# Rows of x as pairs of rounded products with 128 stationary columns, and smaller loads of q, k and v per step

## Chip, cores and metric

One core of a Trainium2 chip runs the whole kernel in one launch. The metric is the device time of a run in microseconds (us). The kernel before was timed in three runs, and one further execution was profiled.

## What is computed

Talking-heads attention over 8 batches, 12 heads, 448 positions and 64 values per head, whose output, laid out as 3584 tokens of 768 values (x), goes through a mixture of 8 experts with one expert chosen for each token:

```python
scores = scale * np.matmul(q, k.transpose(0, 1, 3, 2))
scores = np.einsum('bhij,hg->bgij', scores, w_pre)
scores = scores - np.max(scores, axis=-1, keepdims=True)
attn = np.exp(scores)
attn = attn / (np.sum(attn, axis=-1, keepdims=True) + 1e-09)
attn = np.einsum('bhij,hg->bgij', attn, w_post)
attn_out = np.matmul(attn, v)
x = attn_out.transpose(0, 2, 1, 3).reshape(B * S, H * D)
logits = x @ w_gate
expert_idx = np.argmax(logits, axis=1)
gate_w = softmax(logits)[np.arange(N), expert_idx]
out[expert_idx == e] = gate_w * (np.maximum(xe @ w1[e], 0.0) @ w2[e])
```

## The kernel before

**Two stages.** Attention fills the first 690 us or so and the experts the rest. The attention stage goes over 32 tiles (T) of 120 queries, four to a batch (120, 120, 120 and 88 queries). A tile is cut into blocks of 20 queries, 6 to a tile and 5 to the short one, so there are 184 blocks (NU), 23 to a batch. The program is unrolled in steps u = 0 to 183, one block to a step. A table, `steps`, says which piece of work is issued in which step and stage, and ORDER (L773) gives the order of the stages inside a step. Every engine takes its instructions in that order, SP's and POOL's queues of transfers included.

**One block.** relayout (L286) brings 20 queries of all heads onto 120 partitions by two transfers, two steps ahead. mix (L293) multiplies with w_pre on PE into two PSUM banks (bank_m). maxima (L306) reduces each bank on DVE, and powers (L313) takes the exponentials on ACT with the sums, two instructions and two read-outs. One step later recip (DVE) and weigh (L329, POOL) make w_post divided by the sums, in a buffer wp with three copies. Two steps later post (L338) multiplies with it on PE and turns the block, and evict_p copies it on DVE.

**One tile.** load_q (L125) brings the queries with two transfers, and split_q rounds them to fp32r on ACT (the high part) and subtracts the rounded from the whole on POOL (the low part); load_k and split_k do the same to the keys of the next batch. An fp32r value keeps fewer bits, and PE multiplies it in one go; a product of high and low parts stands for a full one. qk (L260) makes the scores from three such products. av and av_side (L378 to L413) multiply with v, evict_side (ACT) and evict_x (L415, DVE) add the two parts up to x transposed: XT, 128 partitions (two heads) by three chunks by 120 tokens, for each half g of the heads.

**Rows of x.** rows (L425) turns XT round. For each of the six chunks of 128 values, the chunk is the stationary operand (128 x 120 or 128 x 88, fp32), and the moving one is xg, 136 columns: the identity, which gives the tokens as rows, and the 8 columns of w_gate that belong to the chunk, which gives the chunk's share of the logits. evict_r (L433) copies each half, 408 columns, on ACT, store_x writes the rows to the table XD in DRAM with one transfer for each half, and choose (L454) adds the six shares of the logits on DVE and looks for the largest. Its followers (mark, rank, gate, place, token, number, scatter) put the token's number into the list of its expert.

The steps that matter to the change are set in the lines L680 to L756: for the tile before the current one, av in step u0 + 3 and u0 + 5, evict_x one step after each, rows in step u0 + n + 1 (rsteps, n blocks in the current tile), evict_r one later. Loads of q, k and v are issued from L696, L706 and L708. Just ahead of the steps, constants_last (L230) fills constants on POOL; keep_clock (L189) gives PE products of no use to the result while it waits at the start and at the end of the stage.

**Experts.** For each expert, the tokens of its list are gathered from XD, turned and split, and hidden (L1120) and result (L1140) multiply in fp32r with w1 and w2, 512 or 384 moving columns to a product, 128 stationary ones. The change doesn't touch them. patch (L527), at the end of the attention stage, makes four products of 128 stationary columns and a single moving one.

## Time and profile before

| | |
|---|---|
| median of 3 runs | 1230.86 us (1229.25 to 1233.55) |
| the profiled execution | 1217.47 us |
| its span, first to last instruction | 1215.8 us |
| PE busy | 1184.5 us (97%), 19433 matmul records |
| weight loads of PE busy | 995.1 us (82%) |
| DVE, ACT, POOL busy | 798.6, 721.6, 393.4 us |
| TensorE clock granted, mean | 0.994 of full speed |
| moved by DMA | 211.19 MB, 178761 packets |

The profile is of one execution. PE stands for the matmuls, PEld for the loads of their stationary operand, which can go on beside a matmul. One fp32 product stands as two matmul records with a load each, an fp32r product as one. Records of consecutive matmuls overlap, since each is counted to the end of its pipeline: how fast they follow one another is read from starts, and the busy time tells only that PE had something in flight.

### The profile page before, as it was taken

What the parts mean: (1) busy time and instruction counts of PE and PEld (TensorE: products, weight loads), DVE (VectorE), ACT (ScalarE), POOL (GpSimd) and SP (SyncE); (2) the same over time, 40 slices, a digit from 0 to 9 for tenths busy, and PEclk for the clock granted to TensorE, in tenths of its full rate; (3) what the DMA queues carried; (4) which work ended last, traced back from release to release, by engine and by line L of the source; (5) the groups of instructions that cost most, each with busy time, mean ns of one, the idle gap of its engine ahead of it and who ended that gap; (6) DMA issues with size and microseconds to landing.
All of it is one profiled execution on the core that took longest, in us unless ns stands there. A gap on an engine that the chain in (4) does not pass through costs nothing. (4 is left out here: it accounts for less than half of the span.)

```text
span 1215.8 us, 46340 instructions
## 1 busy us (share of the span) xinstructions
PE 1184.5 (97%) x19433; PEld 995.1 (82%) x19433; DVE 798.6 (66%) x1992; ACT 721.6 (59%) x1485; POOL 393.4 (32%) x613
## 2 busy tenths in 40 slices
PE   7999999999999999999999899999999999999996
PEld 3677787777777778777777798898989899989886
DVE  5787888878888878788789745454535344545320
ACT  5777777877777868787776444444434344444220
POOL 5443553534544435445435312020202002110100
PEclk9999999999999999999999999999999999999998
DMA  7566657566656575576556377575555647574300
GB/s 205 191 189 191 200 162 217 181 178 204 204 166 207 157 223 182 171 209 202 175 176 192 108 229 205 166 204 159 181 154 152 170 130 216 166 221 135 120 20 34
DMA packets 178761, 211.19 MB, mean 174 GB/s; under 512 B 85541, under 2 KB 156213, under 8 KB 178536
## 3 DMA queue, kind: packets, MB, share of 16 engines
q1 hardware_dynamic: 172342, 183.93, 51.4%
q0 software_dynamic: 6064, 23.86, 5.6%
q8 instruction: 164, 2.69, 0.9%
q14 instruction: 61, 0.50, 0.1%
q10 hardware_dynamic: 130, 0.22, 0.0%
HBM read 97.59 MB, written 23.07 MB: 99 GB/s over the span
## 5 line engine op out<-in xcount | busy, mean ns | idle before, releaser
L317 ACT ACTIVATE et<-bm,st 124x448 f32<-124x448 f32 x360 | 225.4, 631 | 148.7 <-DVE st L309 123.4
L309 DVE TENSOR_REDUCE st<-bm 124x1 f32<-124x448 f32 x360 | 208.6, 620 | 74.3 <-PE bm L303 68.2
L350 PEld LDWEIGHTS bp<-wp,et 64*64 64x64 f32 (+1 forms) x10052 | 197.0, 135 | 70.0 <-issue 44.8
L1130 PE MATMUL pm_h<-si,ah 128*128 128x512 f32 (+1 forms) x768 | 230.2, 381 | 3.2 <-DVE si L632 2.1
L368 DVE COPY pt<-bp 128x480 f32<-128x480 f32 x352 | 213.6, 649 | 2.4 <-PE bp L350 2.1
L334 POOL TENSOR_SCALAR wp<-Wpost,st 124x60 f32<-124x60 f32 x360 | 151.6, 436 | 164.6 <-DVE st L327 129.1
L350 PE MATMUL bp<-wp,et 64*64 64x60 f32 (+1 forms) x10052 | 190.7, 218 | 0.3 <-issue 0.3
L303 PE MATMUL bm<-sb,Wquad 60*60 60x448 f32 (+3 forms) x1408 | 185.2, 561 | 5.2 <-ACT et L317 5.1
L1130 PEld LDWEIGHTS pm_h<-si,ah 128*128 128x128 f32 x768 | 143.2, 188 | 29.1 <-issue 3.4
L280 ACT COPY si<-bs 120x896 f32<-120x896 f32 (+1 forms) x187 | 159.8, 910 | 6.2 <-PE bs L270 5.8
L1130 PE MATMUL pm_h<-si,al 128*128 128x512 f32 (+1 forms) x384 | 146.0, 380 | 0.0
L1134 DVE SCALAR_TENSOR_TENSOR hl<-pm_h,hh 128x512 fp32r<-128x512 f32 (+1 forms) x64 | 42.1, 658 | 142.7 <-ACT hh L1133 142.6
L410 PE MATMUL bs<-pt,vt 128*64 128x120 f32 (+1 forms) x2496 | 132.5, 262 | 1.2 <-DVE pos L509 1.2
L410 PEld LDWEIGHTS bs<-pt,vt 128*64 128x64 f32 x2496 | 120.0, 138 | 5.3 <-ACT ah L574 1.4
L1133 ACT ACTIVATE hh<-pm_h 128x512 fp32r<-128x512 f32 (+1 forms) x64 | 36.6, 572 | 146.4 <-PE pm_h L1130 146.4
L1150 PE MATMUL pm_y<-bh,hh 128*128 128x384 f32 x480 | 122.1, 334 | 1.3 <-DVE y L1155 1.3
L1150 PE MATMUL pm_y<-bl,hh 128*128 128x384 f32 x480 | 121.8, 334 | 0.0
L148 POOL TENSOR_TENSOR ql<-qr,qh 128x360 fp32r<-128x360 f32 (+1 forms) x78 | 69.8, 905 | 160.9 <-ACT qh L147 123.1
L1150 PE MATMUL pm_y<-bh,hl 128*128 128x384 f32 x480 | 121.8, 334 | 0.0
L648 POOL DMA_INDIRECT si<-XD,tcl x28 | 39.1, 1397 | 254.0 <-DVE y L1155 241.0
L1159 POOL DMA_INDIRECT out<-y,ti x30 | 31.1, 1038 | 184.7 <-ACT y L1157 77.7
L1150 PEld LDWEIGHTS pm_y<-bh,hh 128*128 128x128 f32 x480 | 86.8, 188 | 2.1 <-DVE y L1155 1.6
(170 smaller groups left out, 1723.6 us busy)
## 6 DMA issues: line engine op xcount, KB each, us to landing
sb<-si SPq DMA_DIRECT2D x343, 210.0 KB
wraw<-in_w SPq DMA_DIRECT2D x48, 512.0 KB
wraw<-in_w SPq DMA_DIRECT2D x64, 384.0 KB
vt<-in_v SPq DMA_DIRECT2D x64, 192.0 KB
kr<-in_kT SPq DMA_DIRECT2D x42, 224.0 KB
qr<-in_qT SPq DMA_DIRECT2D x48, 180.0 KB
XD<-xr SPq DMA_DIRECT2D x48, 180.0 KB
sb<-si SPq DMA_DIRECT2D x16, 189.0 KB
```

What stands on the lines that cost most here:

```text
L148: engine.tensor_sub(out=lo, in0=src, in1=hi.bitcast(F32))
L280: copy(out=SI[T][:ni, 2 * c:2 * c + 2, :], in_=bank[:ni, :, :S])
L303: nc.tensor.matmul(out=bank_m[r][CUT[c], :S], lhsT=Wquad[CUT[r], CUT[c]], rhs=sb[CUT[r], c, :], start=True, stop=True)
L309: nc.vector.reduce_max(out=st[:R1, 0, c:c + 1], in_=bank_m[c][:R1, :S], axis=AX.X, negate=True)
L317: nc.scalar.activation(out=et[:R1, c, :], in_=bank_m[c][:R1, :S], func=AF.Exp, bias=st[:R1, 0, c:c + 1], scale=1.0, accum_out=st[:R1, 1, c ...
L334: nc.gpsimd.tensor_scalar(out=wp[:R1, c, :], in0=Wpost[:R1], scalar1=st[:R1, 2, c:c + 1], scalar2=None, op0=ALU.mult)
L350: nc.tensor.matmul(out=banks[r][col * JC:(col + 1) * JC, at_:at_ + W], lhsT=et[CUT[r], n, kg * JC:(kg + 1) * JC], rhs=wp[CUT[r], n, :], st ...
L368: nc.vector.tensor_copy(out=flat[:, :, i0 + r * IB:i0 + (r + 1) * IB] .rearrange("p x (n k) -> p x n k", k=IQ), in_=banks[r][:, :2 * NJ * ...
L410: nc.tensor.matmul(out=HOME[T, g][r * D:(r + 1) * D, p, :], lhsT=VV[b][:, c, h * D:(h + 1) * D], rhs=PT[T][:, c, h, :ni], start=(c == 0), ...
L1130: nc.tensor.matmul(out=ph[:, :n], lhsT=wx[:, fs], rhs=xx, start=(m == 0), stop=(m == 3 * NK1 - 1))
L1134: nc.vector.scalar_tensor_tensor(out=hl[:, ft, :n], in0=ph[:, :n], scalar=0.0, in1=hh[:, ft, :n].bitcast(F32), op0=ALU.max, op1=ALU.subtract)
L1150: nc.tensor.matmul(out=py[g][:, :384], lhsT=hx[:, kt, ts], rhs=wx[:, g * 384:(g + 1) * 384], start=(n == 0), stop=(n == 3 * NK2 - 1))
```

## The change

rows of a tile becomes twelve fp32r products in place of six fp32 ones, for the tiles in PARTED (29 of 32). split_r rounds XT to a high part on ACT and subtracts it on POOL to a low part. Both lie in buffers with eight columns more than the three chunks need, so that a chunk always gives 128 stationary columns. The moving operand xp holds, for two chunks, the identity between the high and low parts of w_gate: 144 columns meet the high part of x, 136 the low part, and both add up in PSUM. A sheet so has 432 columns in place of 408, the rows of two chunks lie side by side in it, and choose adds 96 values for each token in place of 48. To make room, idle has 256 columns in place of 512 with twice as many products, and wp two copies in place of three. load_q comes in two parts in two steps, and loads of k and v are put into other steps; xg, which the three last tiles still use, gets its identity in step 38.

```diff
+XW = P + 2 * NE
-    def load_q(T):
+    def load_q(T, part):
         b, it, ni = geom[T][:3]
-        qr = q_p.tile([P, NPAIR, IT], F32, name="qr", bufs=1)
+        if part == 0:
+            QR[T] = q_p.tile([P, NPAIR, IT], F32, name="qr", bufs=1)
+        cs = slice(part * 3, part * 3 + 3)
...
-            nc.sync.dma_start(out=qr[half * D:(half + 1) * D, :, :ni], in_=src[half])
-        QR[T] = qr
+            nc.sync.dma_start(out=QR[T][half * D:(half + 1) * D, cs, :ni], in_=src[half][:, cs])
...
-    idle = const.tile([P, 512], BF16, name="idle")
+    idle = const.tile([P, 256], BF16, name="idle")
+    xp = r_p.tile([P, NPAIR // 2, 2 * XW - P], F32R, name="xp")
+    XH = [[r_p.tile([P, 3 * IT + 8], F32R, name=f"x{x}{g}") for x in "hl"] for g in range(2)]
...
-        for _ in range(n):
-            nc.tensor.matmul(out=bank, lhsT=idle[:, :P], rhs=idle, start=True, stop=True)
+        for _ in range(2 * n):
+            nc.tensor.matmul(out=bank[:, :256], lhsT=idle[:, :P], rhs=idle, start=True, stop=True)
...
     def constants_last():
-        for c in range(NPAIR):
-            nc.gpsimd.tensor_copy(out=xg[:, c, :P], in_=ident)
+        for p in range(NPAIR // 2):
+            nc.gpsimd.tensor_copy(out=xp[:, p, 2 * NE:XW], in_=ident)
+            for c, (hi, lo) in zip((2 * p, 2 * p + 1), ((NE, 0), (XW, XW + NE))):
+                hi, lo = (xp[:, p, x:x + NE] for x in (hi, lo))
+                nc.vector.tensor_copy(out=hi, in_=xg[:, c, P:XG])
+                nc.vector.tensor_sub(out=lo, in0=xg[:, c, P:XG], in1=hi.bitcast(F32))
+        for x in XH[0] + XH[1]:
+            nc.vector.tensor_copy(out=x[:, 3 * IT:], in_=step.to_broadcast([P, 8]))
...
+    def constants_late():
+        for c in range(NPAIR):
+            nc.gpsimd.tensor_copy(out=xg[:, c, :P], in_=ident)
...
-        wp = e_p.tile([P, 2, H * IQ], F32, name="wp")
+        wp = e_p.tile([P, 2, H * IQ], F32, name="wp", bufs=2)
...
+    def split_r(T, g):
+        ni = geom[T][2]
+        xt = XT.pop((T, g))
+        xh, xl = (x[:, :3 * IT].rearrange("p (c i) -> p c i", i=IT)[:, :, :ni] for x in XH[g])
+        nc.scalar.copy(out=xh, in_=xt[:, :, :ni])
+        nc.gpsimd.tensor_sub(out=xl, in0=xt[:, :, :ni], in1=xh.bitcast(F32))
+
     def rows(T, g, bank):
         ni = geom[T][2]
+        if T in PARTED:
+            SHEET[T, g] = bank[:ni, :3 * XW]
+            for c in range(3):
+                p, odd = divmod(3 * g + c, 2)
+                whole = xp[:, p, odd * 2 * NE:odd * 2 * NE + XW]
+                out = bank[:, c * XW:(c + 1) * XW]
+                cols = slice(0, XG) if odd else slice(NE, XW)
+                xh, xl = (x[:, c * IT:c * IT + P] for x in XH[g])
+                nc.tensor.matmul(out=out, lhsT=xh, rhs=whole, start=True, stop=False)
+                nc.tensor.matmul(out=out[:, cols], lhsT=xl, rhs=whole[:, cols],
+                                 start=False, stop=True)
+            return
...
     def store_x(T, halves=(0, 1)):
...
+        if T in PARTED:
+            ps = slice(2 * halves[0], 2 + halves[-1])
+            nc.sync.dma_start(
+                out=XD[1 + t0:1 + t0 + ni, 2 * P * ps.start:2 * P * ps.stop]
+                .rearrange("t (p x) -> t p x", x=2 * P),
+                in_=XF[T][:ni].rearrange("t (p x) -> t p x", x=2 * XW)[:, ps, 2 * NE:2 * XW - 2 * NE])
+            return
...
+    PARTED = {T for T in rsteps if rsteps[T] <= NU - 9}
...
-            at(max(up - 1, 0), "load", load_q, T)
             for part in range(2):
+                at(max(up - 1, 0) + part, "load", load_q, T, part)
...
-            for part, k in enumerate((16, 17, 19, 20, 22, 24, 25, 27)):
+            for part, k in enumerate((8, 14, 18, 19, 20, 21, 24, 25)):
                 at(u0 + k, "load", load_v, b + 1, part)
-            for c in range(NPAIR):
-                at(U - 18 + 2 * c, "load", load_k, b + 1, c)
+            for c, k in enumerate((6, 7, 9, 11, 13, 15)):
+                at(U - 23 + k, "load", load_k, b + 1, c)
...
             at(vs[g] + 1, "vec", evict_x, T, g)
+            if T in PARTED:
+                at(vs[g] + 1, "early", split_r, T, g)
...
+    at(38, "scatter", constants_late)
```

Three places of the order in which the engines get their instructions. PE, the step in which the first tile's rows are made; before, six fp32 products in one row (bs is a PSUM bank, xt the transposed x, xg the identity with w_gate):

```order
L350 MATMUL bp_106<-wp,et 64x60 x2
L350 MATMUL bp_107<-wp,et 64x60 x2
L430 MATMUL bs_103<-xg,xt 120x136 x6
L303 MATMUL bm_104<-sb_124,Wquad 64x448
L303 MATMUL bm_104<-sb_124,Wquad 60x448
```

The same place now (xh and xl are the high and low part, L457 and L458 the two products):

```order
L365 MATMUL bp_109<-wp,et 64x60 x2
L365 MATMUL bp_110<-wp,et 64x60 x2
L457 MATMUL bs_106<-xp,xh_131 128x144
L458 MATMUL bs_106<-xp,xl_132 128x136
L457 MATMUL bs_106<-xp,xh_131 128x144
L458 MATMUL bs_106<-xp,xl_132 128x136
L457 MATMUL bs_106<-xp,xh_131 128x144
L458 MATMUL bs_106<-xp,xl_132 128x136
L457 MATMUL bs_106<-xp,xh_133 128x144
L458 MATMUL bs_106<-xp,xl_134 128x136
L457 MATMUL bs_106<-xp,xh_133 128x144
L458 MATMUL bs_106<-xp,xl_134 128x136
```

Twelve products take the place of six, between the same neighbours. DVE, from the last copies of the start to the first maximum; before:

```order
L228 MEMSET bp_106 128x512
L228 MEMSET bp_107 128x512
L280 COPY si<-bs_102 120x896
L309 TENSOR_REDUCE st<-bm_104 124x1
L309 TENSOR_REDUCE st<-bm_105 124x1
L325 TENSOR_SCALAR st<-st 124x2
```

Now, from the last of six pairs of small instructions on (the first five pairs read the same):

```order
L240 CAST xp<-xg 128x8
L241 TENSOR_TENSOR xp<-xg,xp 128x8
L243 CAST xh_131<-step 128x8
L243 CAST xl_132<-step 128x8
L243 CAST xh_133<-step 128x8
L243 CAST xl_134<-step 128x8
L324 TENSOR_REDUCE st<-bm_107 124x1
L324 TENSOR_REDUCE st<-bm_108 124x1
L340 TENSOR_SCALAR st<-st 124x2
```

Sixteen instructions stand ahead of the first maximum that did not stand there. POOL, over two steps in which keys are split and x is split too; before:

```order
L334 TENSOR_SCALAR wp<-Wpost,st 124x60 x2
L122 TENSOR_TENSOR kl<-kr,kh 128x448
L334 TENSOR_SCALAR wp<-Wpost,st 124x60 x4
L122 TENSOR_TENSOR kl<-kr,kh 128x448
L549 DMA TB<-tg,di 28672x2
```

and now:

```order
L349 TENSOR_SCALAR wp<-Wpost,st 124x60 x2
L124 TENSOR_TENSOR kl<-kr,kh 128x448
L445 TENSOR_TENSOR xl_132<-xt,xh_131 128x360
L349 TENSOR_SCALAR wp<-Wpost,st 124x60 x4
L124 TENSOR_TENSOR kl<-kr,kh 128x448
L445 TENSOR_TENSOR xl_134<-xt,xh_133 128x360
L599 DMA TB<-tg,di 28672x2
```

The subtraction for x stands behind that for the keys, and ahead of the scatter.

## Rows read from the trace of the kernel before

**Rows 1.** Busy us of each engine (count), PE clock, DMA share, GB/s; attention.
```profile
300.00:400.00 100.00, 99.99 (x2550) 78.95 (x2546) 84.45 (x252) 77.83 (x189) 48.10 (x82) 1.00 0.64 194
```
**Rows 2.** Timeline of PE, one step: start us, us, engine, line, operation, count.
```profile
393.79 1.08 PE L303 MATMUL bm<-sb,Wquad 64*64 64x448 f32 x8
394.59 1.09 PE L350 MATMUL bp<-wp,et 64*64 64x60 f32 x56
...
395.70 1.63 PE L430 MATMUL bs<-xg,xt 128*120 128x136 f32 x12
397.26 0.98 PE L303 MATMUL bm<-sb,Wquad 64*64 64x448 f32 x8
```
**Rows 3.** Timeline of ACT over the same and the next step.
```profile
389.93 0.58 ACT L121 CAST kh<-kr 128x448 fp32r<-128x448 f32 x1
392.51 0.64 ACT L317 ACTIVATE et<-bm,st 124x448 f32<-124x448 f32 x1 [2.00 <-DVE st L309]
...
396.76 0.20 ACT L317 ACTIVATION_READ_ACCUMULATOR et<-bm,st 124x1 f32 x1
...
397.75 0.93 ACT L437 COPY xr<-bs 120x408 f32<-120x408 f32 x2
398.58 0.57 ACT L121 CAST kh<-kr 128x448 fp32r<-128x448 f32 x1
399.09 0.64 ACT L317 ACTIVATE et<-bm,st 124x448 f32<-124x448 f32 x1
```
**Rows 4.** Groups by line and form: count, busy us, mean ns, idle us before.
```profile
L430 PE MATMUL bs<-xg,xt 128*120 128x136 f32 x288 | 39.3, 286 | 0.1
...
L430 PEld LDWEIGHTS bs<-xg,xt 128*120 128x120 f32 x288 | 34.6, 183 | 0.9
```
**Rows 5.** Timeline of PE's weight loads in the rows step.
```profile
395.68 1.44 PEld L430 LDWEIGHTS bs<-xg,xt 128*120 128x120 f32 x12
```
**Rows 6.** Timeline of PE, two experts: first and last start of 21 and of 23 triples.
```profile
702.97 0.51 PE L1130 MATMUL pm_h<-si,ah 128*128 128x384 f32 x2
...
715.11 0.34 PE L1130 MATMUL pm_h<-si,ah 128*128 128x384 f32 x1
...
1149.72 0.62 PE L1130 MATMUL pm_h<-si,ah 128*128 128x512 f32 x2
...
1164.36 0.39 PE L1130 MATMUL pm_h<-si,ah 128*128 128x512 f32 x1
```
**Rows 7.** The products of patch(): ns min/median/max of a load; their timeline.
```profile
L530 PEld LDWEIGHTS bs<-edge,et x4: 186/190/192, 685.0 to 685.4; 120*128 120x128 f32 x4
...
685.02 0.52 PEld L530 LDWEIGHTS bs<-edge,et 120*128 120x128 f32 x4 [1.68 <-DVE si L632]
```
**Rows 8.** Groups by line and form: fp32r weight loads of the experts.
```profile
L1150 PEld LDWEIGHTS pm_y<-bh,hh 128*128 128x128 f32 x480 | 86.8, 188 | 2.1 <-DVE y L1155 1.6
```
**Rows 9.** Groups by line and form: roundings on ACT, a subtraction on POOL.
```profile
L122 POOL TENSOR_TENSOR kl<-kr,kh 128x448 fp32r<-128x448 f32 x42 | 48.4, 1153 | 0.0
...
L147 ACT CAST qh<-qr 128x360 fp32r<-128x360 f32 x48 | 39.7, 827 | 6.6 <-DMA qr<-in_qT 3.9 <-DMA sb<-si 2.8
```
**Rows 10.** Timeline of DVE, the step before the rows step.
```profile
390.87 0.53 DVE L419 TENSOR_TENSOR xt<-bs,xt 128x360 f32<-128x360 f32 x1
```
**Rows 11.** Timeline of POOL, the same step.
```profile
391.73 1.14 POOL L122 TENSOR_TENSOR kl<-kr,kh 128x448 fp32r<-128x448 f32 x1
393.32 1.05 POOL L549 DMA_INDIRECT TB<-tg,di  x1 [0.45 <-DVE tg L544]
394.75 0.84 POOL L334 TENSOR_SCALAR wp<-Wpost,st 124x60 f32<-124x60 f32 x2 [0.39 <-PE bm L303]
```
**Rows 12.** Timeline of DVE at the start of the steps.
```profile
21.21 1.16 DVE L309 TENSOR_REDUCE st<-bm 124x1 f32<-124x448 f32 x2 [1.42 <-PE bm L303]
...
23.45 0.17 DVE L327 RECIPROCAL st<-st 124x2 f32<-124x2 f32 x1
```
**Rows 13.** Groups by line and form: loads of the mix, and what ended their waits.
```profile
L303 PEld LDWEIGHTS bm<-sb,Wquad 64*60 64x60 f32 x352 | 31.8, 128 | 0.9 <-DMA sb<-si 0.8
```

More of the change, by code (lines that the diff above doesn't have):

```diff
@@ L82, in attn_moe_kernel @@
     q_p = kq.enter_context(tc.tile_pool(name="qp", bufs=2, side="right"))
+    r_p = kq.enter_context(tc.tile_pool(name="rp", bufs=1, side="right"))
     att = ctx.enter_context(ExitStack())
@@ L421, in evict_x @@
             nc.vector.tensor_copy(out=xt, in_=home)
-    XR, LG, DD = {}, {}, {}
+    XR, XF, DD = {}, {}, {}
+    def split_r(T, g):
[4 more added lines that the diff above has]
+        nc.gpsimd.tensor_sub(out=xl, in0=xt[:, :, :ni], in1=xh.bitcast(F32))
     def rows(T, g, bank):
         ni = geom[T][2]
+        if T in PARTED:
[10 more added lines that the diff above has]
+            return
         xt = XT.pop((T, g))
@@ L435, in evict_r @@
         if g == 0:
-            XR[T] = x_p.tile([IT, NPAIR, XG], F32, name="xr", bufs=2)
+            XF[T] = x_p.tile([IT, NPAIR * XW], F32, name="xr", bufs=2)
+            XR[T] = XF[T][:, :NPAIR * XG].rearrange("p (c x) -> p c x", x=XG)
+        if T in PARTED:
+            nc.scalar.copy(out=XF[T][:ni, 3 * g * XW:(3 * g + 3) * XW], in_=SHEET.pop((T, g)))
+            return
         nc.scalar.copy(out=XR[T][:ni, 3 * g:3 * g + 3, :], in_=SHEET.pop((T, g)))
@@ L441, in store_x @@
         t0 = b * S + it * IT
+        if T in PARTED:
[4 more added lines that the diff above has]
+                in_=XF[T][:ni].rearrange("t (p x) -> t p x", x=2 * XW)[:, ps, 2 * NE:2 * XW - 2 * NE])
+            return
         for n in halves:
@@ L456, in choose @@
         lg = sm_p.tile([IT, NE], F32, name="lgs")
-        nc.vector.reduce_sum(out=lg[:ni], in_=XR[T][:ni, :, P:XG].rearrange("p c e -> p e c"),
-                             axis=AX.X)
+        if T in PARTED:
+            parts_ = XF[T][:ni].rearrange("q (p w t e) -> q p w t e", p=NPAIR // 2, t=2, e=NE)
+            nc.vector.reduce_sum(out=lg[:ni], in_=parts_[:, :, ::XW // NE - 1].rearrange(
+                "q p s t e -> q e p s t"), axis=AX.XYZ)
+        else:
+            nc.vector.reduce_sum(out=lg[:ni], in_=XR[T][:ni, :, P:XG].rearrange("p c e -> p e c"),
+                                 axis=AX.X)
         m8 = sm_p.tile([IT, NE], F32, name="m8")
@@ L719, in attn_moe_kernel @@
             at(vs[g] + 1, "vec", evict_x, T, g)
+            if T in PARTED:
+                at(vs[g] + 1, "early", split_r, T, g)
             at(r, "rows", rows, T, g, bank_s[1][:, g, :])
@@ L779, in attn_moe_kernel @@
     load_k(0, 1)
-    load_q(0)
+    for part in range(2):
+        load_q(0, part)
     for c in range(2, NPAIR):
@@ L794, in attn_moe_kernel @@
     split_q(0, 1, nc.vector)
-    load_q(1)
+    for part in range(2):
+        load_q(1, part)
     split_k(0, 3, nc.vector)
```

## Prediction

> **What bounds the kernel now.** I read the page first, then the table by stage. [...] A busy PE need not be a bound, so next comes PE's timeline over one of the 184 steps. The step that begins with the mix at 393.79 ends with the next mix at 397.26, and what lies between is matmuls: mix 0.80 us, post 1.0 us, a short rank, and the twelve records of rows(), from 395.70 to the next mix, 1.56 us [rows 2]. The reader is to see that no gap stands between these starts: the mix follows the last record of rows at once.
>
> The third view shows that this is only half of the truth. In the same step ACT reads out its last exponential at 396.76 + 0.20 = 396.96, which is 3.17 us after the mix, and a mix writes over what those exponentials read [rows 3]. So a step can't be much shorter than some 3.15 us, whatever PE does; this one, at 3.47, has 0.3 us to spare. One step later nothing is left: between 397.75 and 399.15 ACT copies both sheets of rows (0.93) and rounds a piece of k (0.57), and its exponential starts at 399.09, with no idle time noted ahead of it [rows 3]. The exponential normally starts 1.83 us after the mix; 397.26 + 1.83 = 399.09 too. ACT is there just in time.
>
> **The change part by part.**
>
> *The products of rows.* 29 of the 32 tiles change over (those whose rows step lies at least nine steps before the end). A tile has six fp32 products now, and each stands in the trace as two records, so twelve: 192 products are 288 + 96 records, of which [rows 4] shows the larger form. In the change a tile has twelve products of one record each. The count of records stays, and the question is what one record takes.
> Before: twelve weight loads take 1.44 us from the first start to the last end and one lasts 0.183, so they follow each other every (1.44 - 0.18)/11 = 0.114 us [rows 4, 5]. The load of 120 columns is hidden there: the matmul is the longer of the two.
> After: an fp32r matmul's time is read from the expert stage. 21 triples of 512 columns take 1164.36 - 1149.72 us, 0.232 us each; 23 triples of 384 columns take 715.11 - 702.97, 0.176 each [rows 6]. That is 0.44 ns a column and 7 ns besides, so 0.070 us for 144 columns and 0.067 for 136 (an estimate; no fp32r product of fewer than 384 columns is in this trace). But each product loads 128 columns of its own. The four products of patch() have one or no more column to stream, so they show the load alone: 128 columns, 0.52 us for four loads, one lasting 0.190, so (0.52 - 0.19)/3 = 0.110 us from one to the next [rows 7]. An fp32r load of 128 columns lasts 0.188, the same [rows 8]. The new product is bound by its load at 0.110. The lower bound is the matmul alone, 0.070; the upper one is load and matmul one after the other, 0.180. I take 0.110: a load goes on beside the matmul before it in [rows 5], and in the expert stage too, where 0.188 us of load stand against a product every 0.176.
> Sum for a tile: eleven distances by 4 ns less, 0.04; the last product streams for 0.067 in place of 0.114, 0.05 less; the first load has eight columns more, 0.01. That is 0.08 us, and by 29 tiles 2.3 us of PE time.
>
> *What feeds them.* split_r adds two ACT roundings and two POOL subtractions of 128x360 to a tile, 58 each. The nearest rows are 128x448: 0.58 us on ACT and 1.15 on POOL; with 360 columns in another order ACT takes 0.83 [rows 3, 9]. So 0.5 to 0.8 us on ACT, and about 0.95 on POOL. Cover: the sums of x, which split_r reads, end at 390.87 + 0.53 = 391.40; ACT is idle for 2.00 us until 392.51 [rows 3, 10], so the rounding fits even at 0.8. POOL has k's subtraction from 391.73 to 392.87 and a scatter from 393.32 [rows 11]; the new 0.95 us between them moves the scatter by 0.5 and the next weigh by 0.1, and post wants that weigh only in the step after. The low part is ready at 393.82, and rows wants it from 395.70 on. Cost nothing; without the cover it would be the 0.3 us of the last rival. wp with two buffers in place of three waits for the post of the step before, which ends ahead of the next mix: nothing.
>
> *What ACT takes back.* The sheets grow from 408 to 432 columns, some 0.05 us for two copies. In the step after rows ACT is just in time, as read above, and rows ends 0.08 earlier: the exponential is then 0.13 us late against PE, and the next mix waits for it. This holds for the two of four rows steps in a batch that are followed by rounding a piece of k. 0.1 us by two by 7 batches: 1.4 us given back.
>
> *The start.* DVE gets 16 small instructions ahead of its first maximum. By the nearest row they take 0.17 us each, 2.7 us, and DVE idles for 1.42 there [rows 12], so at most 1.3 us. Against it, the first half of q needs two smaller transfers and may land up to half a microsecond sooner. Between -0.5 and +1.3, I take +0.5.
>
> *Loads, stores, clock.* q, k and v move by steps on SP's queue and XD gets runs of 1 KB in place of 512 bytes. The mix reads what the relayouts bring, and the one wait for a transfer that a row of its weight loads lists is 0.8 us over the whole run [rows 13]; so the spreading has next to nothing to win on the path, and a relayout that comes later has the two steps of its lead. The reduce over 96 in place of 48 values lies in DVE's waits. keep_clock streams the same columns in twice as many matmuls.
>
> Sum: -2.3 + 1.4 + 0.5 = -0.4 us. The profiled execution would take 1217.47 - 0.4 = 1217.1; the median of the runs, 1230.86, stands 13.4 above it, so 1230.5. About 0.3% (3.7 us) is what can be told from no change.
>
> **Rivals.**
> *Quick weight loads.* If the 128 columns load faster, the products follow every 0.070 us: 11 x 0.044 + 0.05 = 0.53 less a tile, 15.6 us in all. ACT's chain caps it: a step can't fall under some 3.15, and in the two just-in-time places nothing is left. With 0.14 and 0.33 us gained in the other two rows steps of a batch it is about 3.4, so from 1215 to 1228, and I say 1226. Against it: the fp32r load of 128 columns lasts as long as the fp32 one [rows 7, 8].
> [...]
>
> *Short fp32r products at four passes.* This one ends on the other side. [...] If with 144 columns fp32r took what fp32 takes, two records' worth (0.114 x 2 x 140/136 = 0.235), a tile would have 12 x 0.235 = 2.82 in place of 1.37, 1.45 more, 42 us by 29: 1273. It decides from 0.118 us a product on. Nothing speaks for it but the missing rows.
>
> *The load exposed.* If a load that is longer than its matmul can't go on beside it, a product takes 0.180: 29 x 12 x 0.066 = 23 us more, 1254.
>
> *Low parts late.* If POOL's subtraction isn't done when rows begins, PE waits: 0.3 us by two steps in a batch, some 5 us, 1235.
>
> **Chances.** Forecast 0.66 (its own range 1227 to 1234: start, give-back, and up to 3 us of small stalls in the steps that the spread loads may take away); quick loads 0.13; four passes 0.07; exposed 0.05; late 0.09. Faster by over 0.3%: half of the quick loads and 0.13 of the forecast, 0.20. Slower: 0.12 for the two dear rivals, 0.05 of the late one, 0.03 of the forecast, 0.20. Within: 0.60. The range 1223 to 1236 holds the forecast, most of the quick loads and the late case, and leaves out the two dear ones.
>
> **What would show it.** In the changed profile twelve records of rows should follow every 0.11 us with loads of 0.188, and the group should take some 1.48 us to the next mix; ACT's exponential after rows should start about 1.95 after its mix; DVE's first maximum should start half a microsecond late or more. Products every 0.07 with shorter loads prove the first rival, every 0.23 the second, every 0.18 the third. A wait of PE's rows for POOL proves the last. The forecast is wrong if the attention stage's end moves by more than 3.7 us.

## The result, and the profile after

The changed kernel takes 1238.02 us (median of 8 runs, 1236.19 to 1245.06), the kernel before 1228.24 beside it (8 runs). The medians differ by 9.8 us. The ratio, taken from runs side by side, is 1.0096, interval 1.0073 to 1.0119, or 11.8 us (9.0 to 14.6). Forecast were 1230.5 and no measurable difference. The profiled execution of the change has a span of 1234.5 us, that of before had 1215.8; the latter's time of 1217.47 lies below every timed run of that kernel, so by the timed runs only ten to twelve of these 18.7 us are the change. The loss lies in the attention stage: its last mix starts at 691.10 us in place of 673.71, and what follows takes 543.4 and 542.1. Which chip took this result is not on record.

A batch has 23 steps; "position 13" is the step with that number in a batch, counted from 0. The step of [rows 2] is position 13 of the fifth batch. First the table by stage of the changed kernel, which answers [rows 1]: DVE has 1.4 us more, ACT 4, POOL 7.7, in 100.

```profile
300.00:400.00 100.00, 99.78 (x2566) 78.35 (x2567) 85.86 (x250) 81.80 (x198) 55.76 (x91) 1.00 0.63 187
```

PE's timeline of that step, which answers [rows 2] (start, us, engine, line, operation, count):

```profile
401.01 1.03 PE L318 MATMUL bm<-sb,Wquad 64*64 64x448 f32 x8
401.81 0.74 PE L365 MATMUL bp<-wp,et 64*64 64x60 f32 x34
402.73 0.61 PE L365 MATMUL bp<-wp,et 64*64 64x60 f32 x22 [0.18 <-issue]
...
403.35 0.31 PE L457 MATMUL bs<-xp,xh 128*128 128x144 f32 x1
...
404.62 0.27 PE L458 MATMUL bs<-xp,xl 128*128 128x136 f32 x1
404.82 0.98 PE L318 MATMUL bm<-sb,Wquad 64*64 64x448 f32 x8
```

The products are as forecast: eleven distances from 403.35 to 404.62, 0.115 each, and 1.47 us to the next mix (1.56 before). New is a hole in post, that is, a stop of PE inside a group that should run through: its 56 records stop after 34 and go on 0.4 us later, with no semaphore named. Post ends late, and the step takes 3.81 in place of 3.47.

The groups by line, for what feeds the products (busy us, mean ns, idle before):

```profile
L445 POOL TENSOR_TENSOR xl<-xt,xh 128x360 fp32r<-128x360 f32 x44 | 42.3, 969 | 7.5 <-ACT xh L444 7.5
L458 PEld LDWEIGHTS bs<-xp,xl 128*128 128x128 f32 x174 | 33.4, 192 | 0.0
L444 ACT CAST xh<-xt 128x360 fp32r<-128x360 f32 x44 | 21.3, 492 | 37.2 <-DVE xt L434 37.2
L504 DVE TENSOR_REDUCE lgs<-xr 120x8 f32<-120x96 f32 x22 | 7.1, 322 | 0.0
```

POOL around that step, which answers [rows 11]; ahead of it the mix of position 12, before and now:

```profile
390.68 0.98 PE L303 MATMUL bm<-sb,Wquad 64*64 64x448 f32 x8
```
```profile
397.91 0.98 PE L318 MATMUL bm<-sb,Wquad 64*64 64x448 f32 x8
```
```profile
399.03 1.14 POOL L124 TENSOR_TENSOR kl<-kr,kh 128x448 fp32r<-128x448 f32 x1
400.12 0.98 POOL L445 TENSOR_TENSOR xl<-xt,xh 128x360 fp32r<-128x360 f32 x1
401.30 1.04 POOL L599 DMA_INDIRECT TB<-tg,di  x1 [0.19 <-issue]
402.39 0.84 POOL L349 TENSOR_SCALAR wp<-Wpost,st 124x60 f32<-124x60 f32 x2
```

The subtraction takes 0.97 us, as estimated. But the scatter begins 3.39 us after the mix of position 12 (401.30 - 397.91) where before it began 2.64 after (393.32 - 390.68): it has slipped into the rows step, where it runs beside post.

DVE, POOL and ACT of the changed kernel at position 4 of the same batch, one fence an engine; the mix stands at 369.43:

```profile
369.56 1.12 DVE L340 TENSOR_SCALAR st<-st 124x2 f32<-124x2 f32 x1
...
371.13 1.15 DVE L324 TENSOR_REDUCE st<-bm 124x1 f32<-124x448 f32 x2
```
```profile
369.51 1.15 POOL L151 TENSOR_TENSOR ql<-qr,qh 128x360 fp32r<-128x360 f32 x1 [2.29 <-ACT qh L150]
```
```profile
371.84 0.64 ACT L332 ACTIVATE et<-bm,st 124x448 f32<-124x448 f32 x1 [0.18 <-DVE st L324]
```

And the same two instructions in the kernel before, DVE and POOL (mix at 362.63):

```profile
362.80 0.15 DVE L325 TENSOR_SCALAR st<-st 124x2 f32<-124x2 f32 x1
```
```profile
362.84 1.15 POOL L148 TENSOR_TENSOR ql<-qr,qh 128x360 fp32r<-128x360 f32 x1 [2.40 <-ACT qh L147]
```

Before, recip's add starts 0.04 us ahead of POOL's subtraction of q and takes 0.15. Now it starts 0.05 behind it and takes 1.12: both end near 370.67. DVE's maximum is then late, ACT's exponential starts 2.41 after the mix in place of 1.83, and the next mix waits for ACT. Positions 4 and 5 take 3.28 and 4.26 us (medians of six batches) in place of 3.13 and 3.78.

The kernel before has such holds too, where nothing waited for them. Its DVE and POOL at 236 us:

```profile
236.03 0.57 DVE L325 TENSOR_SCALAR st<-st 124x2 f32<-124x2 f32 x1
```
```profile
235.42 1.16 POOL L122 TENSOR_TENSOR kl<-kr,kh 128x448 fp32r<-128x448 f32 x1
```

Of the 184 adds of recip 28 take over 0.25 us in the first trace of before, 41 in that of the change.

The start, DVE and POOL, which answers [rows 12]:

```profile
20.58 0.17 DVE L240 CAST xp<-xg 128x8 fp32r<-128x8 f32 x1
20.78 1.17 DVE L241 TENSOR_TENSOR xp<-xg,xp 128x8 fp32r<-128x8 f32 x1
...
22.79 1.14 DVE L324 TENSOR_REDUCE st<-bm 124x1 f32<-124x448 f32 x2
```
```profile
20.76 1.18 POOL L151 TENSOR_TENSOR ql<-qr,qh 128x360 fp32r<-128x360 f32 x1 [2.87 <-ACT qh L150]
```

One of the 16 small instructions is held in the same way, 1.17 for 0.17, and the first maximum starts at 22.79 where it was 21.21. The first step takes 4.29 in place of 2.48. How much of that stays is less clear: the granted clock stands at 0.50 of full speed for 3.4 us in the first trace of before (from 27.1 us) and for 6.8 in that of the change (from 26.4), and the first ten steps together take 36.5, 36.5 and 35.2 us in the three traces of the change (the result, runs 9 and 13), 34.0 and 36.0 in the two of before.

### The profile page after: what moved, and what is told of

It is laid out like the page before. It is cut to its first block, busy times and chain, and to the rows that moved or that the text cites. A ratio compares the mean times of both kernels' runs of the same rounds, so it can differ in the third digit from the quotient of the medians.

```text
span 1234.5 us, 46552 instructions
## 1 busy us (share of the span) xinstructions
PE 1194.1 (97%) x19458; PEld 1001.0 (81%) x19458; DVE 816.1 (66%) x2008; ACT 750.3 (61%) x1543; POOL 445.2 (36%) x674
## 5 line engine op out<-in xcount | busy, mean ns | idle before, releaser
L365 PEld LDWEIGHTS bp<-wp,et 60*64 60x64 f32 (+1 forms) x10052 | 198.7, 135 | 81.2 <-issue 68.9
L365 PE MATMUL bp<-wp,et 60*64 60x60 f32 (+1 forms) x10052 | 196.4, 219 | 6.2 <-issue 6.0
L318 PE MATMUL bm<-sb,Wquad 64*64 64x448 f32 (+3 forms) x1408 | 186.5, 563 | 7.4 <-ACT et L332 7.4
```

What stands on the lines that cost most here:

```text
L318: nc.tensor.matmul(out=bank_m[r][CUT[c], :S], lhsT=Wquad[CUT[r], CUT[c]], rhs=sb[CUT[r], c, :], start=True, stop=True)
L365: nc.tensor.matmul(out=banks[r][col * JC:(col + 1) * JC, at_:at_ + W], lhsT=et[CUT[r], n, kg * JC:(kg + 1) * JC], rhs=wp[CUT[r], n, :], st ...
```

## The experiments

Five series, each on one chip with runs of the kernel before beside it (medians 1228.69, 1226.62, 1224.90, 1227.08, 1228.67). The second was on another chip than the first, the third and fourth on one chip, the fifth on another. Microseconds against the kernel before, below, are the ratio less 1 times that median.

| run | kernel | ratio, interval |
|---|---|---|
| 1 | change, no low part | 1.0034, 1.0008 to 1.0060 |
| 2 | change, old loads | 1.0069, 1.0037 to 1.0101 |
| 3 | change, low part behind the scatter | 1.0078, 1.0047 to 1.0110 |
| 4 | before + split_r, wp, keep_clock | 1.0030, 1.0005 to 1.0055 |
| 5 | change, no add in recip | 1.0033, 1.0008 to 1.0058 |
| 6 | change, start's instructions later | 1.0023, 1.0002 to 1.0044 |
| 7 | change, k a step later | 1.0060, 1.0039 to 1.0080 |
| 8 | before + keep_clock | 1.0020, 0.9995 to 1.0045 |
| 9 | the change again | 1.0035, 1.0002 to 1.0068 |
| 10 | before again | a single execution, 1226.86 us |
| 11 | as 6 | 1.0047, 1.0018 to 1.0076 |
| 12 | 5, 6 and 7 together | 1.0036, 1.0007 to 1.0065 |
| 13 | the change, third time | 1.0060, 1.0033 to 1.0087 |
| 14 | 5 and 6 together | 1.0013, 0.9986 to 1.0040 |
| 15 | 14 with old loads | 0.9983, 0.9953 to 1.0013 |
| 16 | before + new loads | 1.0003, 0.9976 to 1.0030 |
| 17 | 15 again | 1.0034, 1.0014 to 1.0055 |
| 18 | 5 again | 1.0046, 1.0024 to 1.0068 |

The steps, as medians over six batches of the time from mix to mix; step 0 and step 182 are single steps of the whole run:

| trace | pos. 0 | 1 | 3 | 4 | 5 | 13 | 14 | 19 | step 0 | step 182 |
|---|---|---|---|---|---|---|---|---|---|---|
| before | 3.12 | 3.28 | 3.89 | 3.13 | 3.78 | 3.48 | 3.11 | 3.46 | 2.48 | 4.07 |
| change | 3.36 | 2.94 | 3.98 | 3.28 | 4.26 | 3.73 | 3.11 | 3.77 | 4.29 | 6.21 |
| 1 | 3.13 | 3.13 | 3.76 | 3.35 | 4.29 | 3.33 | 3.11 | 3.34 | 5.01 | 7.87 |
| 3 | 3.12 | 3.13 | 3.76 | 3.33 | 4.29 | 3.33 | 3.55 | 3.32 | 3.24 | 6.24 |
| 4 | 3.38 | 3.04 | 4.48 | 3.23 | 3.76 | 3.76 | 3.10 | 3.79 | 2.48 | 6.24 |
| 5 | 3.13 | 3.13 | 4.31 | 3.39 | 3.74 | 3.33 | 3.10 | 3.31 | 4.31 | 4.07 |
| 9 (change) | 3.13 | 3.12 | 4.37 | 3.35 | 4.18 | 3.33 | 3.11 | 3.32 | 4.18 | 4.08 |
| 10 (before) | 3.12 | 3.28 | 3.77 | 3.13 | 3.77 | 3.47 | 3.11 | 3.42 | 2.48 | 4.07 |
| 13 (change) | 3.13 | 3.12 | 4.54 | 3.23 | 4.16 | 3.33 | 3.09 | 3.31 | 4.29 | 4.07 |
| 14 | 3.12 | 3.13 | 4.43 | 3.18 | 3.75 | 3.33 | 3.10 | 3.32 | 2.48 | 4.07 |
| 16 | 3.12 | 3.28 | 3.78 | 3.14 | 3.77 | 3.48 | 3.11 | 3.47 | 2.48 | 4.07 |
| 17 | 3.27 | 3.01 | 3.74 | 3.44 | 3.75 | 3.37 | 3.11 | 3.40 | 2.48 | 6.11 |
| 18 | 3.59 | 2.94 | 4.30 | 3.69 | 3.77 | 3.44 | 3.10 | 3.38 | 3.24 | 6.00 |

**First series: feeding and loads.** Run 1 takes out POOL's new subtraction, so it leaves the low part of x out of the result; run 2 puts the loads back, run 3 moves the subtraction. Run 4 is the kernel before with split_r, its results unused, and with the change's two buffers for wp and its keep_clock. The diffs show only the lines that matter.

```diff
 # run 1, in split_r
-        nc.gpsimd.tensor_sub(out=xl, in0=xt[:, :, :ni], in1=xh.bitcast(F32))
 # run 2
-            for part, k in enumerate((8, 14, 18, 19, 20, 21, 24, 25)):
+            for part, k in enumerate((16, 17, 19, 20, 22, 24, 25, 27)):
 # and k's and q's loads as before
 # run 3: the subtraction in a stage of its own
-             "choose", "token", "qk", "evict_s", "side", "split", "scatter", "split_w")
+             "choose", "token", "qk", "evict_s", "side", "split", "scatter", "lows", "split_w")
 # run 4, in the kernel before (wp and keep_clock as in the change)
+                at(vs[g] + 1, "early", split_r, T, g)
```

> The change without POOL's subtraction: the low part of x stays zero (so the low part of the rows of x is left out of the result), the products and all else are unchanged. Theory A (the 58 subtractions on POOL cost the time: they push POOL's scatter into the next step and hold DVE's recip until they end): 8 to 11 us less than the change, so 1227 to 1230, ratio to the kernel before 0.999 to 1.002. Theory B (the moved loads of q, k and v cost the time, by way of PE's instruction fetches or late relayouts): no less than 1236, ratio 1.007 to 1.010. Theory C (rounded products are no faster in the step and the start costs the rest): 1236 too.

> The change with the loads of q, k and v in the steps and pieces of before. Theory A: stays within 2 us of the change, 1236 to 1240, ratio 1.007 to 1.011. Theory B: most of the 10 us comes back, 1228 to 1231, ratio 1.000 to 1.003, and the two long stops of PE inside post (1.38 and 2.59 us in the changed kernel's trace) are gone.

> The change with POOL's subtraction put behind the scatter in its step in place of ahead of it. Theory A: the scatter begins 2.6 us after its step's mix again, as before, and post takes 0.8 us again in the steps with rows; 3 to 6 us less than the change, 1232 to 1235, ratio 1.003 to 1.006; the holds of recip may stay or move. Theory B: no change, 1236 to 1240.

> The kernel before with only the new work of split_r added (ACT's rounding and POOL's subtraction, 29 tiles, results unused), wp with two buffers and the shorter idle tile; products, loads and start as before. Theory A: 8 to 12 us over the kernel before, ratio 1.006 to 1.010. Theory B and C: within 2 us of the kernel before, ratio 0.999 to 1.002.

Measured: +4.2, +8.5, +9.6 and +3.7 us against the kernel before. The change itself was not timed in this series. Run 1 is 7.6 us under the change's 11.8 of the first result; run 4 shows 3.7, but keep_clock alone shows 2.5 (run 8, -0.6 to 5.5), so what the feeding costs by itself is not separated. Run 1 lies between what its theories A and B forecast, run 4 too; run 2 fits A. Runs 2 and 3 can't be told from the change: their intervals overlap its. The traces are sharper. In runs 1 and 3 the scatter runs ahead of post again and post has no hole (positions 13 and 19 at 3.33); in run 4, which has the old products, the holes are there (3.76, 3.79). Run 3's trace, PE and POOL in its rows step:

```profile
404.65 1.03 PE L318 MATMUL bm<-sb,Wquad 64*64 64x448 f32 x8
405.46 1.04 PE L365 MATMUL bp<-wp,et 64*64 64x60 f32 x56
```
```profile
404.19 1.04 POOL L603 DMA_INDIRECT TB<-tg,di  x1 [0.37 <-DVE tg L598]
405.27 0.96 POOL L449 TENSOR_TENSOR xl<-xt,xh 128x360 fp32r<-128x360 f32 x1
```

Post is whole beside the subtraction; it is the scatter beside post that goes with the hole. Theory A of run 3 so had the scatter and post right and the time wrong (1.0078 for 1.003 to 1.006): position 14 takes 3.55 now, and DVE's holds behind POOL grow: 55 of recip's adds take over 0.25 us, 36 us more than 0.15 each, where the change's trace has 41 and 19 us.

**Second series: the places one by one.**

```diff
 # run 5, recip
-        nc.vector.tensor_scalar(out=st[:R1, 2, :nh], in0=st[:R1, 1, :nh], scalar1=1e-9,
-                                scalar2=None, op0=ALU.add)
-        nc.vector.reciprocal(out=st[:R1, 2, :nh], in_=st[:R1, 2, :nh])
+        nc.vector.reciprocal(out=st[:R1, 2, :nh], in_=st[:R1, 1, :nh])
 # run 6: out of constants_last, on nc.gpsimd
+    for p in range(NPAIR // 2):
+        at(3 + 2 * p, "scatter", constants_pair, p)
 # run 7
-            for c, k in enumerate((6, 7, 9, 11, 13, 15)):
+            for c, k in enumerate((7, 8, 10, 12, 14, 16)):
-                at(U - 15 + 2 * c, "early", split_k, b + 1, c)
+                at(U - 14 + 2 * c, "early", split_k, b + 1, c)
 # run 8: keep_clock of the change in the kernel before
```

> The change without the add of 1e-9 in recip (a sum that is 1 or more does not move by it), so that DVE has no tensor_scalar there that POOL's subtraction of q can hold. Theory 1 (choose's longer reduce puts recip's add behind POOL's subtraction, which holds it for 0.95 us; the maxima, the exponentials and so the second half of the next mix come 0.5 us late): the two steps of a batch that take 3.3 and 4.29 us take 3.13 and 3.77 again, 4 to 5 us less than the change over seven batches, 1233 to 1234.5, ratio to the kernel before 1.004 to 1.0055. Rival (the 0.5 us comes from late relayouts or from PE itself): those steps stay at 4.29 and the time at 1236 or more but for some 0.1 us a step on DVE that nothing waits for.

> The change with the 16 small instructions on the gate's weights and the tails moved from DVE's start to POOL's steps 3 to 7. Theory (they stand ahead of the first maximum on DVE and delay the second step): the first step takes 2.5 us in place of 4.3 again, 1.5 to 2.5 us less than the change, 1235 to 1236.5, ratio 1.006 to 1.007. Rival (the start is as long by the loads of q): no change, 1237 to 1239.

> The change with each piece of k loaded and split one step later, so that no step has k's subtraction, a scatter, a weigh and the new subtraction on POOL together. Theory 2 (POOL is overfull by 0.9 us in the two steps of a batch ahead of rows, and the scatter that slips into the next step stops PE inside post for 0.2 to 0.5 us): post takes 0.8 us again in the steps with rows at the batch's positions 13 and 19, these steps 3.33 in place of 3.75, some 0.8 us a batch, 4 to 6 us less than the change, 1232 to 1234, ratio 1.003 to 1.005. Rival (the stop in post has another cause than POOL's queue): 1236 to 1240.

> The kernel before with keep_clock alone changed (the same columns in twice as many matmuls, 44 more instructions in PE's program ahead of the attention stage, nothing else moved). Theory 4 (PE's instructions come in blocks of 256, and the shift by 44 moves the place where PE runs out): the step before the last of the attention stage takes 6.2 us in place of 4.07, and the time is 1 to 3 us over the kernel before, ratio 1.001 to 1.0025. Rival (what is new there comes from split_r or wp): that step stays at 4.07 and the ratio within 0.999 to 1.001.

In run 5 the hold is gone. Its DVE and POOL at the same place:

```profile
372.01 0.15 DVE L340 RECIPROCAL st<-st 124x2 f32<-124x2 f32 x1
```
```profile
371.96 1.13 POOL L151 TENSOR_TENSOR ql<-qr,qh 128x360 fp32r<-128x360 f32 x1 [3.10 <-ACT qh L150]
```

The reciprocal starts 0.05 us behind POOL's subtraction, as the add did, and takes 0.15; position 5 is 3.74. So it is the add that is held. Theory 1 forecast both steps back to normal: position 4 stays at 3.39, so only position 5's excess is shown to be recip's. The times of this series could not be set beside the change, which wasn't in it, because the traces of runs 5, 6 and 7 lack the holes in post and have 4.07 or 4.08 in step 182, run 6 too, whose PE program and POOL order in those steps are the change's. So the chip could be behind it. Run 6 came out quicker than forecast (1.0023 for 1.006), and runs 7 and 8 don't decide between their theories: the holes and the 6.2 us that they were to move are in no trace of this chip.

**Third and fourth series: the change itself as the measure.**

> The changed kernel as it is, on the chip of this series, to tell the kernel from the execution and the chip. If the stops of PE inside post (0.2 to 0.5 us in the steps at positions 0, 13 and 19 of a batch) and the 6.2 us of the step before the last belong to the kernel, they stand in this trace too, and the ratio is 1.008 to 1.011. If they belong to the chip or the execution, those steps take 3.13, 3.33, 3.32 and 4.07 us here, and the ratio falls to 1.004 to 1.007.

> The kernel before as it is, for a second profiled execution. If its first one was a lucky one (it lies below every timed run) the trace shows 5 to 13 us of stops of PE where its 256-instruction blocks end, against 1 us in the first trace, and 1223 to 1230 us. If the kernel before really has no such stops, 1216 to 1219.

> The same kernel as in the sixth run (the change with the 16 small instructions moved from DVE's start to POOL's steps 3 to 7), beside the change itself on one chip. If the start is what it gives back: 1.5 to 2.5 us less than the change of this series. If the sixth run's 8 us were the kernel's: 7 to 9 us less, with the stops inside post gone from the trace here and not in the change's.

> The change with the three repairs together: no add in recip, the start's small instructions in POOL's later steps, k loaded and split one step later. If they add up: 3.5 us for recip, 2 us for the start and 3 us for POOL's queue, so 8 to 10 us less than the change, 1226 to 1230, ratio 0.999 to 1.002. If the stops of PE at its instruction blocks set the time, the gains are lost in part, 1230 to 1234.

> The changed kernel once more, as the measure of this series. If the chip decides whether PE stops inside post, either 1.003 to 1.005 (post undisturbed at positions 0, 13 and 19) or 1.008 to 1.011 (disturbed); nothing between.

> The change with two repairs, no add in recip and the start's small instructions in POOL's later steps; loads as in the change. Theory D (the places that repeat in every batch and the start set the time): 6 to 7 us less than the change of this series. Theory F (PE's instruction fetches, which come late behind the moved loads, take back what is gained): 0 to 2 us less, and stops at the ends of PE's blocks grow to 13 us or more.

> The same two repairs with the loads of q, k and v in the steps and pieces of before. Theory F: the stops at the ends of PE's blocks fall to 5 or 6 us as in the kernel before, and the time lies 2 to 4 us under the kernel before, ratio 0.997 to 0.999. Theory D: the same time as the run with two repairs and new loads, within 1.5 us.

> The kernel before with only the new pieces and steps of the loads of q, k and v. Theory F: stops at the ends of PE's blocks of 10 us or more and 3 to 6 us over the kernel before, ratio 1.003 to 1.005. Theory D: no change, 0.999 to 1.001.

Run 9, the same kernel as the change, PE and POOL in the step of position 13 (the next mix stands at 408.33):

```profile
405.01 1.03 PE L318 MATMUL bm<-sb,Wquad 64*64 64x448 f32 x8
405.81 1.03 PE L365 MATMUL bp<-wp,et 64*64 64x60 f32 x56
...
406.86 0.31 PE L457 MATMUL bs<-xp,xh 128*128 128x144 f32 x1
```
```profile
405.27 1.04 POOL L599 DMA_INDIRECT TB<-tg,di  x1 [0.18 <-issue]
```

The scatter has slipped here too, 0.26 us behind the mix, and post is whole. The holes go with the slipped scatter, and with the chip or the execution: they stand in the traces of the first result and of the first and fifth series, and in none of the three series between. Step 182, whose rows the change leaves as they were, shows the same. PE stops there three times, beside or just behind two transfers of POOL; in run 9 both begin as long after the mix (1.6 and 3.0 us), and PE runs through. The change's PE and POOL, then run 9's:

```profile
686.50 0.90 PE L405 MATMUL bs<-pt,vt 64*64 64x60 f32 x20
687.81 0.35 PE L405 MATMUL bs<-pt,vt 64*64 64x60 f32 x4 [0.41 <-issue]
688.55 0.45 PE L425 MATMUL bs<-pt,vt 128*64 128x120 f32 x4 [0.40 <-issue]
689.29 1.88 PE L425 MATMUL bs<-pt,vt 128*64 128x120 f32 x32 [0.29 <-issue]
691.10 0.64 PE L312 MATMUL bm<-sb,Wpre 124*124 124x448 f32 x1
```
```profile
686.51 1.10 POOL L599 DMA_INDIRECT TB<-tg,di  x1 [0.43 <-DVE tg L594]
687.92 1.05 POOL L698 DMA_INDIRECT si<-XD,ti  x1 [0.30 <-issue]
```
```profile
685.93 0.54 PE L405 MATMUL bs<-pt,vt 64*64 64x60 f32 x24
686.40 2.07 PE L425 MATMUL bs<-pt,vt 128*64 128x120 f32 x36
```
```profile
685.95 1.10 POOL L599 DMA_INDIRECT TB<-tg,di  x1 [0.43 <-DVE tg L594]
```

No trace of the kernel before shows this (4.07 in both), but on the chips of the first and fifth series it was timed and not traced. The change is 4.3 and 7.4 us slower without the holes (runs 9 and 13) and 11.8 with the holes, though run 13's interval and the first one's overlap; run 13's 1.0060 lies where its expectation allowed nothing. Recip's hold and the late start are in both. Both mended bring 5.8 us beside run 13 in the same series (run 14: +1.6, run 13: +7.4; the intervals overlap by 0.0007), and 2.7 beside run 9. The start alone (run 11) shows nothing in the time, and run 12, with all three repairs, is no quicker than the change beside it (1.0036 and 1.0035; 8 to 10 us were forecast). New loads alone cost nothing that run 16 shows (+0.4, -2.9 to +3.7), old loads under the repaired change are 3.7 us better than new ones, within the intervals (run 15). By their medians run 14 is nearest to theory D, run 15 to F and run 16 to D; no interval decides between the two. Run 10, the second trace of before, has a span of 1225.1, so the first one was a quick execution.

**Fifth series.**

> The two repairs with the old loads a second time, to tell whether this version beats the kernel before. If the products' 0.15 us a tile are what is left (some 3.5 us over the attention stage) and PE's late fetches are as before: ratio 0.996 to 0.999. If late fetches take it: 1.000 to 1.002.

> The change without recip's add, beside it on one chip: start as in the change, loads as in the change. If the hold of recip costs 3.5 to 4.5 us and the start 2, this one lies 2 us over a version with both repairs and new loads (1.0013 in the series before), so 1.002 to 1.004; if only the start counts, 1.005 to 1.007; if only recip counts, 1.000 to 1.002.

Run 17 is at +4.2 us, over both of its ranges, and run 18 at +5.7, between two of its. They show position 0 at 3.27 and 3.59 and step 182 at 6.1 and 6.0, so the holes are there again, in run 17 hardly at positions 13 and 19 (3.37 and 3.40), and run 17 can't be pooled with run 15. No version beats the kernel before for certain.

## Why the prediction was wrong, step by step

- **Products: right, and worth more, the parts by luck.** 0.110 was forecast, 0.115 measured, loads of 0.188 against 0.192, 1.48 us for the group against 1.47. The steps at positions 1, 7, 13 and 19 take 0.16, 0.07, 0.15 and 0.14 us less where post is whole (run 9 against before): 0.52 a batch, 3.6 us in seven, where 2.3 was put down. In position 13, 0.09 of the 0.15 is the group; 0.06 lies ahead of it (post's start to the first product 1.05 in place of 1.11). The group's 0.09 is close to the forecast 0.08, but from other parts: before, the matmuls of positions 13 and 19 follow each other every 0.123 us by their own starts, not every 0.114 as read from the loads, so the eleven distances bring 0.08 and the last product 0.01, where 0.04 and 0.05 were put down. The three rivals on the products fell: no load quickened (0.192), no product took the 0.235 us of two fp32 records, none waited for its load (0.115 a product, not 0.180). "Four passes" is the author's name for that figure; no trace shows passes.
- **"What ACT takes back", 1.4 us: right in one of two places, 0.6.** ACT in run 9 behind the mix at 408.33, and before behind that at 397.26:

```profile
410.25 0.63 ACT L332 ACTIVATE et<-bm,st 124x448 f32<-124x448 f32 x1
410.87 0.63 ACT L332 ACTIVATE et<-bm,st 124x448 f32<-124x448 f32 x1
```
```profile
399.71 0.63 ACT L317 ACTIVATE et<-bm,st 124x448 f32<-124x448 f32 x1
```

  The exponential starts 1.92 us after its mix, as forecast (1.95), and the second one ends at 3.17 in place of 3.08. The step still takes 3.11, but the next one, position 15, pays: the third record of its mix starts 0.20 us after the first in place of 0.12, and the step takes 4.25 to 4.28 in place of 4.17 where nothing else disturbs it (4.16 in the last batch, which has no next keys to round). Seven times 0.09 is 0.6 us. At the other place, positions 8 and 9, nothing is given back (position 9 takes 4.15 undisturbed in both kernels).
- **"Cost nothing" for the feeding: wrong.** The sizes were right (0.49 and 0.97 us). It said that the subtraction "moves the scatter by 0.5 and the next weigh by 0.1" and asked only whether the results are ready. They are; measured are 0.75 and 0.42 (402.39 - 401.01 in place of 394.75 - 393.79). What counts is beside what the slipped scatter then runs. In the change's first trace the positions 0, 1, 2, 13 and 19 are together 1.07 us longer than in run 9 (medians: 0.23 - 0.18 + 0.17 + 0.40 + 0.45), 7.5 us in seven batches. The last rival had the place and the engine, but another mechanism: PE waits for no low part (0.0 us idle ahead of L458's 174 loads).
- **"The reduce over 96 in place of 48 values lies in DVE's waits": wrong.** It takes 0.32 in place of 0.23, and the order of two starts that were 0.04 us apart turned over. Positions 4 and 5 pay 0.15 + 0.48 us a batch in the change, 0.10 to 0.22 and 0.38 to 0.41 in runs 13 and 9: 3.4 to 4.4 us in seven, 2.7 to 3.4 of them at position 5, the part that run 5 shows to be recip's. Run 4 has the add, the new work and the old sheets, and no hold at position 5; runs 1 and 2 have the hold. So it comes with the new sheets and choose, not with the feeding or the loads. On DVE the reduce, three short instructions on its result and the add follow one another: from the start of the reduce to that of the add it was 0.63 us before (362.17 to 362.80) and is 0.71 now (368.85 to 369.56); with 0.08 less the add would still start 0.03 ahead of POOL.
- **The start, "+0.5", at most 1.3: too small.** The bound counted 16 instructions against DVE's idle time and left out that POOL can hold one (1.17 us for 0.17). That half of q may land half a microsecond sooner was the author's estimate, which no row showed; in the change's trace its first rounding starts at 5.34 us in place of 6.44, and the second at 7.78 in place of 7.53. The first step is 1.7 to 1.8 us longer in every trace of the change, but over the first ten steps less may be left, as said above.
- **Loads "next to nothing": not contradicted by run 16's time, but not settled.** "A relayout that comes later has the two steps of its lead" is not so everywhere: at position 3 the mix of run 9 waits for a relayout in three of six batches, for 0.98, 0.52 and 0.46 us, and never there in the traces of before. With the old loads such waits stand at position 2 (three of 0.56 to 0.70 us in run 15, one of 1.49 in run 10). The batch of [rows 2] in run 9:

```profile
369.58 0.20 PEld L318 LDWEIGHTS bm<-sb,Wquad 64*60 64x60 f32 x6 [0.52 <-DMA sb<-si]
```

Two terms failed, then, that the prediction put at nothing: the feeding ("cost nothing") and choose's longer reduce ("lies in DVE's waits"). Of both it asked whether there is room and whether the results come in time, and not what they push beside which instruction of POOL. The start was mis-sized besides. The sum without holes is -3.6 + 0.6 + 2.7 to 4.4 + 1.8 = +1.5 to +3.2 us; measured are +4.3 and +7.4, with intervals from +0.2 and +4.0. In the first result position 15 gives nothing back and the holes add 7.5: with 3.4 to 4.4 for recip 9.1 to 10.1, and 11.8 was measured, with an interval from 9.0. Some 1 to 6 us are not accounted for without holes, and about 2 with them, as much as step 182 is longer there. Part of the rest lies at position 3, which takes 3.89 and 3.77 us in the two traces of before and 4.37 and 4.54 in runs 9 and 13, 3.4 to 5.4 us in seven batches: late relayouts, and a stop of another kind that is seen in every trace. In the change's first one, step 118, the clock behind it by the row of 453 to 457 us, and among the DMA queues:

```profile
449.90 0.75 PE L365 MATMUL bp<-wp,et 64*64 64x60 f32 x39
453.02 0.68 PE L365 MATMUL bp<-wp,et 60*64 60x60 f32 x17 [2.37 <-issue]
```
```profile
453.00:457.00 4.00, 3.98 (x69) 3.76 (x68) 2.10 (x8) 0.00 (x0) 1.97 (x3) 0.57 0.71 248
```
```profile
q8 instruction: 164, 2.69, 0.9%
```

PE stops for 2.6 us. Behind the stop the granted clock is at 0.50 of full speed for 3.4 us (0.57 in the mean of that row), so the step takes 7.88 in place of 3.99. Counted in PE's own records, five of the 24 idle times of over 0.1 us between 50 and 690 us come at the same count modulo 256, 193: 0.25 us at 75.2, 1.16 at 284.4, 0.13 at 289.6, 0.50 at 433.0 and the 2.37 at 453.0, the two longest among them. The queue's 164 packets of 16 KB would make 41,984 instructions at 256 each, and PE has 39,361 records in the trace, some being missing: so they are taken to be PE's instructions, an estimate from these counts. The packet ahead of this stop landed 1.5 us before PE went on, as ahead of other such stops of 0.6 us and more in this trace and in those of runs 9 and 13 (1.2 to 1.6). Added up (each gap less the median of the same place in the other batches) they are about 1 to 3 us in the first trace of before and 4 to 5 in its second, 6 in the change's first and 11 to 13 in runs 9 and 13. They are part of why executions of one kernel differ: the attention stage is 9.4 us longer in the second trace of before, and 3 to 4 of these are such stops. In the thirteen traces with the new loads they come to some 6 to 18 us, 13 in the median, in the seven with the old loads to 3 to 14, 5 to 6 in the median. That speaks for the loads as what delays the packets, but it isn't shown to be what the change lost: each trace is one execution, run 16 has 8 to 9 us of them and loses no measurable time, and run 14, with 14, is quick.

What the prediction didn't weigh is that POOL can hold DVE. The traces show 1.12 us for 0.15 and 1.17 for 0.17, each ending with POOL's subtraction, and the reciprocal that isn't held (0.15). In the change's first trace 29 adds of recip begin at least 0.3 us before the end of a subtraction of POOL that began first: 25 of them, begun 0.05 us or more behind its start, take 0.34 to 1.14 us and end within 0.03 of its end; the other four, begun within 0.01 of its start, take 0.15. Of the 184 reciprocals there 14 lie wholly within such a subtraction and 11 within an indirect transfer, and none takes over 0.18. Why these adds are held and the reciprocals are not, no trace shows, and no run gives the holes in post a cause.

## What to carry to other kernels

When work is put on GpSimd "in an idle gap", list every VectorE instruction of that step that starts within its span, and every one that starts as close to a neighbouring GpSimd instruction as the add did here (0.15 us when it began 0.04 ahead, 1.12 when it began 0.05 behind): an order that holds by 0.04 us is not a margin. Follow what is pushed out of the gap to the place where it lands, not only to the moment when its result is wanted. And before a difference under one per cent is explained by two traces, take a second trace of the same kernel, on another chip too. An add of 0.57 us where its neighbours take 0.15 stood in the trace of before: a small instruction that is now and then four times as long is worth a question before the change.

## What the runs showed of the hardware that was not expected

- A 0.15 us VectorE add on 124x2 values took 1.12 us behind a GpSimd subtraction (the change's first trace, 369.56 us); a reciprocal of the same size took 0.15 (run 5, 372.01 us).
- The same program stops PE beside or just behind GpSimd indirect transfers in the change's first trace (0.18 us of idle time listed at 402.73 us, 0.29 to 0.41 at three places in step 182, which takes 6.21) and not in runs 9 and 13 (step 182: 4.08 and 4.07). Runs 4, 17 and 18, on other chips than runs 9 and 13, have the long step as well (6.24, 6.11 and 6.00). Unexplained.
- PE seems to run out of instructions, which is the author's reading of the counts above: single stops of up to 2.6 us, five at the same count modulo 256 in the change's first trace, some 1 to 18 us in all by the execution. The longest one there was followed by 3.4 us at a granted clock of 0.50.
